# One attention, mixture and tanhshrink kernel: the weight decode in two streams, finished tokens kept in DRAM, sums kept in PSUM, later tokens prepared in small steps

## The chip, the cores and the metric

The kernel runs on one core of one Trainium2 chip. The metric is the device time of one execution in microseconds; the kernel before takes 1109.34 us (median of three timed runs, 1107.19 to 1110.84). Engines are named as in the profile: PE (matrix multiply), DVE (vector), ACT (activation), POOL (GpSimd), SP (here only the queue that issues DMAs).

## The reference, cut to what matters

Three stages follow each other. All data are float32, and the last two weight matrices arrive as float64.

```python
# 1: two attentions, 4 batches x 8 heads, 576 tokens, head size 64, 32 packed queries
p_packed = softmax_attention(p, k, v)
x = softmax_attention(q, p_packed, p_packed)      # -> x: 2304 tokens x 512
# 2: mixture of 4 experts, 512 -> 1024 -> 512
for e in range(4):
    out += prob[:, e:e+1] * (relu(x @ w1[e]) @ w2[e])
# 3: tanhshrink network, 512 -> 2048 -> 512; w_in and w_out are float64
h = out @ w_in
result = (h - tanh(h)) @ w_out
```

## The kernel before, in words

Every float32 product is made of three PE products of rounded parts: each operand is split into a high part `h` (an ACT copy that rounds to the format PE reads) and a low part `l` (the rest, a subtraction on DVE or POOL). PE then multiplies high by high, high by low and low by high into one PSUM sum. So each tile that PE is to read costs an ACT instruction and a DVE or POOL instruction first.

**The middle stage** has two passes `p` (two batches, 1152 tokens, 9 token tiles of 128 each) and eight chunks `c` of hidden columns (half an expert each). `pack_w1` (L425, token `W`) folds the packed queries into the up weights, and forms the sums of blocks (`wsum`, `wp`) that a seven-product form of the 2x2 block multiplication needs. `up_prod` (L509, token `g`) makes, for one chunk and one batch, the hidden activations in four steps with two PSUM tiles X and Z (names `hpx`, `hpz`, two banks each, pool `ps2` of two tiles). Step 0 multiplies into X, which ACT copies out, then into Z; `done` (L535) then adds the copy to Z on DVE (L536, `p<-hpz,p`), which writes the sum to SBUF, and `split_h` (L459) applies the relu: ACT writes `h0h` (L461), DVE writes `h0l` (L462). Step 1 goes on summing in X, and begins a new sum in Z (`hpz<-th`). Step 2 does two such `done`s, one of X and one of Z (`u`), step 3 the last piece of X. `down` (L567, token `d`) multiplies one token tile's activations by the down weights, 12 PE products of 512 columns (`yps`), and DVE adds the scaled result to that tile's `x2` (L586), a tile of the 20-buffer pool `u2`. An `x2` tile lives from the first chunk of its pass until the third stage has read it, so in the second pass 18 of the 20 buffers hold `x2`.

**PE's order** is written out by hand as strings of such tokens (`EVEN`, `ODD`, `TURN`, `LASTA`, `LAST`, L60 to L70) and run in that order. DVE, ACT, POOL and SP execute what the planner gave them in the order it laid down at build time, ready work first and earlier program text first among it. Each engine takes its list strictly from the front.

**The decode** (`decode`, L363) turns the float64 bit patterns of `w_in` and `w_out` into float32 pairs and stores them in DRAM (`wing`, `wout_s`) for the third stage. It is one generator; each `_` in the strings adds `STEPS` = 1.3 to a credit, and whole credits are spent on its steps; after a load step the spending stops until the next `_`. For each of 32 blocks of 128x512 words, `words` (L334) runs one ACT copy (L338), two DVE instructions (L339, L343), an ACT square in the same step (L346), two more on DVE (L348, L352) and two on POOL (L354, L355). `w_in` blocks go in pairs through block sums (L372 to L376), then all are split and stored. The work tiles come from the 5-buffer pool `k4`, which also holds the raw down weights (`wraw`, L415) and `wsum`. A group takes two blocks of `w_in` and two of `w_out` in turn, 23 steps, and there are eight groups; the strings hold 156 `_`.

**The third stage** takes three units `u` of 768 tokens. `x_quad` (L619, token `q`) transposes three `x2` tiles for each quarter of the tokens on PE (L638, `xps`), forms the block sums T1 to T4 straight from PSUM (L644) and splits (`x_split`, L610, helper L147 and L148). For unit 0 all four quarters use the one tile of pool `psw`; for units 1 and 2 the quarters are made inside the main loop. That loop has 24 steps n of one column group each: `s3` (L685, `h3ps`) makes the seven products of group n, with ACT copies (L708) and DVE adds (L712) out of two one-bank PSUM tiles; `elem` and `elem_split` do the tanhshrink and the split; `s4` (L924, `ops`) multiplies group n-2 by `w_out` into six one-bank tiles. The quarters of unit 1 stand in step 1, those of unit 2 in steps 9 and 10; three of the seven splits of a unit follow in later steps (`late_split`).

Of the kernel before, what the change touches and what calls it, by code (L numbers as in the profile page):

```python
# [26 lines left out]
STEPS = 1.3  # L27
# [39 lines left out]
    "w0 g7110 _ d710 _ q00 g7111 _ d711 _ g7112 _ q01 d712 g7113 q02 d713 q03 d714 s0 d715 s1 d716 s2 d717 s3 d718 "  # L67
# [4 lines left out]
def kernel(  # L72
# [66 lines left out]
    cst = const.tile([128, 20], F32, name="cst")  # L139
    wing = [dram.tile([128, 2, 1792], F32, name=f"wing{i}") for i in range(8)]  # L140
# [194 lines left out]
    def words(st, lf):  # L335
# [9 lines left out]
        )  # L345
        nc.scalar.activation(out=hw.bitcast(F32), in_=hw.bitcast(F32), func=ACTF.Square)  # L346
# [16 lines left out]
    def decode():  # L363
        for i in range(8):
            w = k4t([128, 2, 512], F32R, "win")
            for b in range(2):
                st = load_words(win[2 * i + b])
                yield True
                yield from words(st, f(w[:, b]))
            a11, a12, a21, a22 = (f(w[:, b, 256 * k:256 * k + 256]) for b in range(2) for k in range(2))  # L370
            s = k4t([128, 4, 256], F32R, "wins")
            nc.vector.tensor_tensor(out=f(s[:, 0]), in0=a21, in1=a22, op=ALU.add)  # L372
            nc.vector.tensor_tensor(out=f(s[:, 1]), in0=f(s[:, 0]), in1=a11, op=ALU.subtract)
            yield
            nc.vector.tensor_tensor(out=f(s[:, 2]), in0=a11, in1=a21, op=ALU.subtract)
            nc.vector.tensor_tensor(out=f(s[:, 3]), in0=a12, in1=f(s[:, 1]), op=ALU.subtract)  # L376
            hi = k4t([128, 1024], F32R, "winh")
            for h, l in ((hi[:, 0:512], w[:, 0]), (hi[:, 512:768], w[:, 1, 256:512])):
                nc.scalar.activation(out=h, in_=f(l), func=ACTF.Copy)
                nc.gpsimd.tensor_tensor(out=l, in0=f(l), in1=f(h), op=ALU.subtract)  # L380
            yield
            nc.sync.dma_start(out=wing[i][:, 0, 0:768], in_=f(hi[:, 0:768]))
            nc.sync.dma_start(out=wing[i][:, 1, 0:512], in_=f(w[:, 0]))
            nc.sync.dma_start(out=wing[i][:, 1, 512:768], in_=f(w[:, 1, 256:512]))
            yield
            hi = k4t([128, 4, 256], F32R, "winh")
            nc.scalar.activation(out=hi, in_=f(s), func=ACTF.Copy)
            for k in (slice(0, 2), slice(2, 4)):
                nc.gpsimd.tensor_tensor(out=s[:, k], in0=f(s[:, k]), in1=f(hi[:, k]), op=ALU.subtract)
            yield  # L390
            for k, t in enumerate((hi, s)):
                nc.sync.dma_start(
                    out=wing[i][:, k, 768:1792], in_=f(t).rearrange("p a b -> p (a b)")
                )
            yield
            for b in range(2):
                st = load_words(wout[2 * i + b])
                yield True
                o = k4t([128, 2, 512], F32R, "fo")
                lf = f(o[:, 1])  # L400
                yield from words(st, lf)
                nc.scalar.activation(out=o[:, 0], in_=lf, func=ACTF.Copy)
                nc.gpsimd.tensor_tensor(out=o[:, 1], in0=lf, in1=f(o[:, 0]), op=ALU.subtract)
                yield
                nc.sync.dma_start(out=wout_s[2 * i + b], in_=f(o))


    w2h, w2l, wph, wpl, raw = {}, {}, {}, {}, {}

# [209 lines left out]
    def x_quad(u, q):  # L619
# [4 lines left out]
        def raw():  # L624
            if u == 0:
                return k4t([128, 2, HT], F32, "xr")
# [412 lines left out]
```

## Time and profile before

| | |
|---|---|
| timed runs, median | 1109.34 us |
| profiled execution, whole | 1105.16 us |
| its span, first to last instruction | 1103.3 us |
| PE busy | 1069.0 us, 97% |
| DVE busy | 877.4 us, 80% |
| ACT busy | 638.3 us, 58% |
| POOL busy | 250.9 us, 23% |
| mean granted clock of PE | 0.995 |

The profile is of one execution. Busy is the time in which an engine had an instruction under way; a wait names the instruction whose end released the waiting one; the granted clock is a share of full speed (1.0 is 2.4 GHz, 0.5 is 1.2 GHz). The ends of PE's products are modelled, so PE may be busy and yet not at its peak. An attention stage fills the first 90 us, the middle stage runs to about 690, the third stage to the end.

### The profile page before, as it was taken

The numbers are of one execution on the slowest core, as the hardware profiler recorded it, in microseconds if no ns is written. First come the engines' busy times: TensorE is split into PE (matmuls) and PEld (weight loads), VectorE is DVE, ScalarE is ACT, GpSimd is POOL, SyncE is SP. The second block draws the span as 40 slices with busy tenths as digits, with TensorE's granted clock in tenths as the row PEclk, the third lists the DMA queues.
The fourth block names the chain that finished last, engine by engine and source line by source line (L and its number), as shares of the span: only waits on it lengthen the run. The fifth ranks groups of instructions, "written<-read, shape, count | busy, mean of one in ns | idle before, by whom it ended". The sixth has DMA issues, their size and how long they took to land.

```text
span 1103.3 us, 16383 instructions
## 1 busy us (share of the span) xinstructions
PE 1069.0 (97%) x6356; PEld 904.5 (82%) x6356; DVE 877.4 (80%) x1327; ACT 638.3 (58%) x1001; POOL 250.9 (23%) x185
## 2 busy tenths in 40 slices
PE   8899999999999999989999998999999899999998
PEld 6777888888778888778887787888999789889886
DVE  4677898888897857888978776799887968778885
ACT  3456454455554455455555443577777757777675
POOL 0102153553544224445445430000000000000000
PEclk9999999999999999999999999999999899999999
DMA  9624224342444222434352413254555435565532
GB/s 343 211 65 158 94 86 151 128 171 93 166 131 168 77 77 78 163 113 143 138 178 90 147 41 134 76 190 173 205 196 200 171 130 205 191 215 187 199 124 96
DMA packets 42317, 162.84 MB, mean 148 GB/s; under 512 B 4736, under 2 KB 5760, under 8 KB 39168
## 3 DMA queue, kind: packets, MB, share of 16 engines
q1 hardware_dynamic: 42240, 161.80, 41.8%
q8 instruction: 50, 0.82, 0.3%
q14 instruction: 27, 0.22, 0.1%
HBM read 133.99 MB, written 27.79 MB: 147 GB/s over the span
## 4 chain that ended last, share of the span: by engine, by line
PE 39%; DVE 6%; ACT 2%; issue 1%; POOL 1%; DMA 1%; DVEq 0%; ACTq 0%; POOLq 0%
PE ops L937 16%; PE h3ps L699 15%; PE yps L575 5%; PE hpx L525 1%; PE hpz L525 1%; DVE xr L644 1%; DVE xl L148 1%; DVE gl L920 0%; PE xps L638 0%; DVE h1l L462 0%; DVE f L348 0%; DMA f<-in_win_dram 0%; DVE x L586 0%; DVE h L898 0%; DMA wout<-fo 0%
## 5 line engine op out<-in xcount | busy, mean ns | idle before, releaser
L937 PE MATMUL ops<-wo,gh 128*128 128x512 f32 x576 | 179.7, 393 | 1.6 <-DVE xr L644 1.5
L423 POOL TENSOR_TENSOR w2l<-wraw,w2h 128x512 fp32r<-128x512 f32 x64 | 94.3, 1494 | 210.5 <-ACT w2h L421 189.5
L937 PEld LDWEIGHTS ops<-wo,gh 128*128 128x128 f32 x576 | 107.2, 189 | 20.9 <-issue 2.3
L575 PE MATMUL yps<-w2h,h0h 128*128 128x512 f32 x288 | 118.1, 410 | 4.4 <-DVE x L586 3.0
L586 DVE SCALAR_TENSOR_TENSOR x<-yps,pn,x 128x512 f32<-128x512 f32 x126 | 93.7, 743 | 30.7 <-PE yps L575 30.3
L937 PE MATMUL ops<-wo,gl 128*128 128x512 f32 x288 | 114.0, 396 | 0.9 <-DVE gl L920 0.9
L575 PE MATMUL yps<-w2h,h0l 128*128 128x512 f32 x288 | 113.6, 395 | 0.0
L575 PE MATMUL yps<-w2l,h0h 128*128 128x512 f32 x288 | 113.3, 393 | 0.0
L575 PE MATMUL yps<-w2h,h1l 128*128 128x512 f32 x288 | 112.5, 391 | 0.6 <-DVE h1l L462 0.6
L575 PE MATMUL yps<-w2h,h1h 128*128 128x512 f32 x288 | 112.9, 392 | 0.0
L575 PE MATMUL yps<-w2l,h1h 128*128 128x512 f32 x288 | 112.2, 390 | 0.0
L699 PE MATMUL h3ps<-xh,wg 128*128 128x384 f32 x384 | 106.5, 337 | 0.6 <-DVE h L712 0.6
L525 PE MATMUL hpx<-th,wp 128*128 128x288 f32 x336 | 81.5, 298 | 4.3 <-DVE p L536 3.6
L575 PEld LDWEIGHTS yps<-w2h,h0h 128*128 128x128 f32 x288 | 54.3, 188 | 37.1 <-issue 21.0
L894 DVE TENSOR_TENSOR t<-h,t 128x768 f32<-128x768 f32 (+1 forms) x50 | 46.2, 924 | 37.9 <-ACT t L892 37.8
L699 PEld LDWEIGHTS h3ps<-xh,wg 128*128 128x128 f32 x384 | 70.3, 188 | 3.1 <-DVE h L712 0.9
L699 PE MATMUL h3ps<-xbh,wg 128*128 128x384 f32 x224 | 64.7, 346 | 5.0 <-DVE h L712 3.8
L889 ACT ACTIVATE z<-h 128x768 f32<-128x768 f32 (+1 forms) x50 | 40.8, 816 | 47.8 <-DVE h L712 47.7
L525 PEld LDWEIGHTS hpx<-th,wp 128*128 128x128 f32 x336 | 58.6, 188 | 9.8 <-DVE p L536 5.2
L575 PEld LDWEIGHTS yps<-w2h,h1l 128*128 128x128 f32 x288 | 54.1, 188 | 13.0 <-DVE h1l L462 1.1
L937 PEld LDWEIGHTS ops<-wo,gl 128*128 128x128 f32 x288 | 54.1, 188 | 12.9 <-DVE gl L920 1.3
L699 PE MATMUL h3ps<-xl,wg 128*128 128x384 f32 x192 | 64.5, 336 | 0.0
(177 smaller groups left out, 2642.0 us busy)
## 6 DMA issues: line engine op xcount, KB each, us to landing
wg<-wing SPq DMA_DIRECT2D x24, 1792.0 KB, 7.2
wraw<-in_w_dram SPq DMA_DIRECT2D x64, 512.0 KB, 4.5
wo<-wout SPq DMA_DIRECT2D x48, 512.0 KB, 5.1
f<-in_win_dram SPq DMA_DIRECT2D x16, 512.0 KB, 4.7
f<-in_wout_dram SPq DMA_DIRECT2D x16, 512.0 KB, 5.0
wout<-fo SPq DMA_DIRECT2D x16, 512.0 KB, 2.9
kt<-in_kT_dram SPq DMA_DIRECT2D x16, 288.0 KB, 5.6
qt<-in_qT_dram SPq DMA_DIRECT2D x16, 288.0 KB, 6.8
```

The source lines that it names most:

```text
L148: (eng or nc.vector).tensor_tensor(out=lo, in0=src, in1=f(hi), op=ALU.subtract)
L423: nc.gpsimd.tensor_tensor(out=l[:, k], in0=r[:, k], in1=f(h[:, k]), op=ALU.subtract)
L525: nc.tensor.matmul(out=ps[:, ff, 0:HB], lhsT=W[a][:, slot, c0], rhs=x[b], start=(start and k == 0), stop=(stop and k == 2), skip_group_che ...
L575: nc.tensor.matmul(out=ps, lhsT=a[:, ff, o:o + 128], rhs=w[c, fp][:, ff], start=(k == 0), stop=(k == 11),)
L586: last[0] = nc.vector.scalar_tensor_tensor(out=x2[tt], in0=ps, scalar=pn[:, tt, e:e + 1], in1=x2[tt], op0=ALU.mult, op1=ALU.add,).ins
L644: nc.vector.tensor_tensor(out=out[:, k], in0=src if a is None else a[:, k], in1=src if b is None else b[:, k], op=ALU.subtract,)
L699: nc.tensor.matmul(out=ps, lhsT=wg[n][:, a, slot, 128 * kk:128 * kk + 128], rhs=x[c][b][kk] if isinstance(x[c][b], list) else x[c][b][:, k ...
L889: nc.scalar.activation(out=zk, in_=hk, func=ACTF.Square)
L894: nc.vector.tensor_tensor(out=tk, in0=hk, in1=tk, op=ALU.subtract)
L937: nc.tensor.matmul(out=ps, lhsT=a, rhs=wo[n][ff][:, w], start=(i == 0 and ff == 0 and k == 0), stop=(i == NG - 1 and ff == 1 and k == 2), ...
```

## The change

Five edits go together.

1. **Decode.** The generator becomes two. Each handles every second block: first the 16 `w_out` blocks, then the 8 groups of `w_in`, 7 steps a block and 20 steps a group, 272 steps in all. Each credit goes to the other stream than the last. `words` yields once more, ahead of the ACT square. Outputs come from `u2`; only the loaded words stay in `k4`. Stores are made piece by piece (`store_split`), in two DMAs each. `STEPS` is 1.9, and a load no longer ends the spending.
2. **Finished tokens.** In the last chunk of pass 0, `down` stores each finished `x2` tile to DRAM (`xs`) and gives its buffer back; `reload` (token `l`) fetches tiles 0 to 5 at the head of `LAST`, and 6 to 8 after `d714`.
3. **Sums in PSUM.** `done` writes its sum over the PSUM tile it came from, and the relu and the split read it there; only the first `done` of step 2 still writes to SBUF, as X goes on summing.
4. **Unit 0.** The fourth quarter's transposes use a `ps2` tile, and the first group's Z uses the `psw` tile. T1 and T2 are now split with the second and third quarter, T4 and T3 with the fourth.
5. **Units 1 and 2.** A quarter is now two `x_raw` calls, each with three transposes and one ACT copy into SBUF; the sums and splits (`x_prep`) are made from there, mostly in place, in five parts over steps 3 to 7 and 11 to 15, each behind the last DVE add of the step before. Step 10 orders its `s4` parts anew.

```diff
-STEPS = 1.3
+STEPS = 1.9
+PREP = (0, 3, 11)
...
-    "w0 g7110 _ d710 _ q00 g7111 _ d711 _ g7112 _ q01 d712 g7113 q02 d713 q03 d714 s0 d715 s1 d716 s2 d717 s3 d718 "
+    "w0 l06 g7110 _ d710 _ q0 g7111 _ d711 _ g7112 _ q1 d712 g7113 q2 d713 q3 d714 l69 s0 d715 s1 d716 s2 d717 s3 d718 "
...
+    xs = [dram.tile([128, 512], F32, name=f"xs{t}") for t in range(TP)]
...
         )
+        yield
         nc.scalar.activation(out=hw.bitcast(F32), in_=hw.bitcast(F32), func=ACTF.Square)
...
+    def store_split(dst, c, t):
+        n = t.shape[-1]
+        hi = u2t([128, n], F32R, "fh")
+        nc.scalar.activation(out=hi, in_=f(t), func=ACTF.Copy)
+        yield
+        nc.gpsimd.tensor_tensor(out=t, in0=f(t), in1=f(hi), op=ALU.subtract)
+        yield
+        nc.sync.dma_start(out=dst[:, 0, c:c + n], in_=f(hi))
+        nc.sync.dma_start(out=dst[:, 1, c:c + n], in_=f(t))
+    def decode_out(blocks):
+        for i in blocks:
+            st = load_words(wout[i])
+            yield
+            t = u2t([128, 512], F32R, "fo")
+            yield from words(st, f(t))
+            yield from store_split(wout_s[i], 0, t)
+    def decode_in(groups):
+        for i in groups:
+            w = []
             for b in range(2):
                 st = load_words(win[2 * i + b])
+                yield
+                w.append(u2t([128, 512], F32R, "fi"))
+                yield from words(st, f(w[b]))
+            a11, a12, a21, a22 = (f(w[b])[:, 256 * k:256 * k + 256] for b in range(2) for k in range(2))
+            sm = [u2t([128, 512], F32R, "fs") for _ in range(2)]
+            s1, s2, s3, s4 = (f(t)[:, 256 * k:256 * k + 256] for t in sm for k in range(2))
+            nc.vector.tensor_tensor(out=s1, in0=a21, in1=a22, op=ALU.add)
+            nc.vector.tensor_tensor(out=s2, in0=s1, in1=a11, op=ALU.subtract)
             yield
+            nc.vector.tensor_tensor(out=s3, in0=a11, in1=a21, op=ALU.subtract)
+            nc.vector.tensor_tensor(out=s4, in0=a12, in1=s2, op=ALU.subtract)
             yield
+            for c, t in ((0, w[0]), (512, w[1][:, 256:512]), (768, sm[0]), (1280, sm[1])):
+                yield from store_split(wing[i], c, t)
+    streams = [
+        itertools.chain(decode_out(range(k, 16, 2)), decode_in(range(k, 8, 2))) for k in range(2)
+    ]
 
...
-        def done(ps, t, fp, half):
-            nc.vector.tensor_tensor(out=t, in0=ps[:, :, 0:HB], in1=t, op=ALU.add)
-            split_h(fp, slice(t0 + half * HB, t0 + half * HB + HB), t)
+        def done(ps, t, fp, half, keep=False):
+            o = t if keep else ps[:, :, 0:HB]
+            nc.vector.tensor_tensor(out=o, in0=ps[:, :, 0:HB], in1=t, op=ALU.add)
+            split_h(fp, slice(t0 + half * HB, t0 + half * HB + HB), o)
-            done(X, p5, 1, 1)
+            done(X, p5, 1, 1, True)
...
+        if p == 0 and c == NCH - 1:
+            nc.sync.dma_start(out=xs[tt], in_=x2.pop(tt))
+
+    def reload(a, b):
+        for t in range(a, b):
+            x2[t] = u2t([128, 512], F32, "x2")
+            nc.sync.dma_start(out=x2[t], in_=xs[t])
...
+        pl, tg = (ps2, "p2") if q == 3 else (psw[0], "pw")
+        ps = pl.tile([128, 2, 512], F32, tag=tg, name="xps")
...
+    RAW = ("B12", "B22", "B11", "B21")
+    def x_raw(u, q, k):
+        c = RAW[q]
+        kh, th = int(c[1]) - 1, int(c[2]) - 1
+        if k == 0:
+            if q < 3:
+                xr[c] = late["raw"].tile([128, 2, HT], F32, tag="xr", name="xr")
+            else:
+                xr[c] = [u2t([128, HT], F32, "xr") for _ in range(2)]
+        ps = late["ops"].tile([128, 512], F32, tag="ops", name="xps")[:, 0:HT]
+        for i in range(3):
+            c0 = 128 * (2 * kh + k)
+            nc.tensor.transpose(
+                ps[:, 128 * i:128 * i + 128], x2[6 * u + 3 * th + i][:, c0:c0 + 128], ident
+            )
+        with tc.high_priority(offset=PRIO):
+            nc.scalar.activation(out=xr[c][k] if q == 3 else xr[c][:, k], in_=ps, func=ACTF.Copy)
+    def x_prep(u, k):
+        if k == 0:
             x_tiles(u)
+            x_split(u, "B11")
+            xr["T1"] = xr["B11"]
+            x_minus("T1", "B12", "B11")
+        elif k == 1:
             x_split(u, "T1")
+            x_split(u, "B22")
+        elif k == 2:
+            xr["T2"], xr["T3"] = xr["T1"], xr["B12"]
+            x_minus("T2", "B22", "T1")
+            x_minus("T3", "B22", "B12")
+            x_split(u, "T2")
+        elif k == 3:
+            x_split(u, "B21")
+            xr["T4"] = xr["B22"]
+            x_minus("T4", "B21", "T2")
+        else:
+            x_split(u, "T4")
+            x_split(u, "T3")
...
-                xz[n] = [ps2.tile([128, 2, 512], F32, tag="p2", name="h3ps")[:, 0, 0:HT] for _ in range(2)]
+                xz[n] = [
+                    pl.tile([128, 2, 512], F32, tag=tg, name="h3ps")[:, 0, 0:HT]
+                    for pl, tg in ((ps2, "p2"), (psw[0], "pw"))
+                ]
...
             while credit[0] >= 1:
                 credit[0] -= 1
-                if next(bg, None):
-                    break
+                next(streams[0], None)
+                streams.reverse()
...
-                order[k].append(("q", 1, k))
+                order[k] += [("r", 1, k, 0), ("r", 1, k, 1)]
         if n == NG + 1:
-            order[2].append(("q", 2, 0))
-            order[3].append(("q", 2, 1))
+            order[2] += [("r", 2, 0, 0), ("r", 2, 0, 1)]
+            order[3] += [("r", 2, 1, 0), ("r", 2, 1, 1)]
         if n == NG + 2:
             order = [
-                [("s", n, 0), ("q", 2, 2)], [("s", n, 1), ("q", 2, 3)],
-                [("s", n, 2), ("o", m, range(0, 4), 0)], [("s", n, 3), ("o", m, range(4, 6), 0), ("o", m, range(6), 1)],
+                [("s", n, 0), ("r", 2, 2, 0), ("r", 2, 2, 1)],
+                [("s", n, 1), ("r", 2, 3, 0), ("r", 2, 3, 1), ("o", m, range(0, 4), 0)],
+                [("s", n, 2), ("o", m, range(4, 6), 0), ("o", m, range(0, 2), 1)], [("s", n, 3), ("o", m, range(2, 6), 1)],
             ]
+        for u in (1, 2):
+            if 0 <= n - PREP[u] < 5:
+                with tc.issue_after(summed[n - 1]):
+                    x_prep(u, n - PREP[u])
```

## Rows read from the trace of the kernel before

**Rows 1.** Windows, by stage: window; us; busy (instructions) of PE, PEld, DVE, ACT, POOL; clock; DMA.

```profile
90.00:640.00 550.00, 536.81 (x3230) 441.92 (x3231) 456.17 (x684) 281.84 (x448) 235.95 (x167) 1.00 0.37 128
...
680.00:700.00 20.00, 16.80 (x80) 14.19 (x79) 15.38 (x22) 8.92 (x15) 0.00 (x0) 0.91 0.25 93
700.00:750.00 50.00, 47.76 (x248) 42.24 (x247) 44.16 (x75) 37.53 (x67) 0.00 (x0) 1.00 0.47 174
...
845.00:880.00 35.00, 30.01 (x143) 26.37 (x142) 30.45 (x48) 28.04 (x45) 0.00 (x0) 0.90 0.55 193
880.00:1090.00 210.00, 210.00 (x1044) 188.56 (x1043) 167.86 (x226) 152.56 (x218) 0.00 (x0) 1.00 0.48 172
```

**Rows 2.** Waits of PE, whole span: who waited for whom: us in total, times, longest.

```profile
PE hpz L525 <- DVE p L536: 5.2, 7, 1.3
...
PE hpx L525 <- DVE p L536: 3.6, 3, 1.9
PE xps L638 <- DVE xl L148: 3.2, 1, 3.2
PE yps L575 <- DVE x L586: 3.0, 4, 1.0
```

**Rows 3.** Windows around one of three spells of low clock.

```profile
860.00:864.40 4.40, 4.22 (x17) 4.12 (x18) 4.40 (x8) 4.40 (x8) 0.00 (x0) 0.61 0.12 45
```

**Rows 4.** Timeline, ACT, one copy of 384 columns out of PSUM.

```profile
715.52 0.49 ACT L653 ACTIVATE xr<-xps 128x384 f32<-128x384 f32 x1 [0.51 <-issue]
```

**Rows 5.** Groups by line, DVE, form by form: line, instruction, count | busy us, mean ns | idle.

```profile
L462 DVE SCALAR_TENSOR_TENSOR h0l<-u,h0h 128x576 fp32r<-128x576 f32 x28 | 30.9, 1104 | 0.2
...
L462 DVE SCALAR_TENSOR_TENSOR h0l<-p,h0h 128x576 fp32r<-128x576 f32 x28 | 25.9, 926 | 10.0 <-ACT h0h L461 9.9
...
L462 DVE SCALAR_TENSOR_TENSOR h1l<-hpx,h1h 128x576 fp32r<-128x576 f32 x28 | 21.0, 751 | 5.3 <-ACT h1h L461 5.1
...
L148 DVE TENSOR_TENSOR xl<-xr,xh 128x768 fp32r<-128x768 f32 x6 | 5.6, 952 | 0.4 <-ACT xh L147 0.4
```

**Rows 6.** DMA issues: tiles, queue, count, KB each, median us from issue to landing.

```profile
wg<-wing SPq DMA_DIRECT2D x24, 1792.0 KB, 7.2
...
out_dram<-po SPq DMA_DIRECT2D x18, 256.0 KB, 2.1
```

**Rows 7.** Timeline, the issue of one DMA on SP's queue.

```profile
562.71 0.33 SPq L415 DMA_DIRECT2D wraw<-in_w_dram  x1
```

**Rows 8.** Line L462: count: shortest/median/longest ns, first and last start, shapes.

```profile
L462 DVE SCALAR_TENSOR_TENSOR h0l<-p,h0h x28: 745/758/1856, 93.7 to 670.8; 128x576 fp32r<-128x576 f32 x28
```

**Rows 9.** Timeline, DVE, 288 to 297 us: start, length, instruction, [idle before <-releaser].

```profile
288.39 0.43 DVE L339 TENSOR_SCALAR f<-f 128x512 uint32<-128x512 uint32 x1 [2.57 <-ACT fo L338]
...
291.86 0.75 DVE L536 TENSOR_TENSOR p<-hpz,p 128x576 f32<-128x576 f32 x1
...
294.68 1.85 DVE L462 SCALAR_TENSOR_TENSOR h0l<-p,h0h 128x576 fp32r<-128x576 f32 x1
```

**Rows 10.** Timeline, POOL, 293 to 296 us.

```profile
294.55 1.37 POOL L355 TENSOR_TENSOR fo<-fo,f 128x512 f32<-128x512 f32 x1
```

**Rows 11.** Timeline, PE, 287 to 293 us.

```profile
287.60 0.30 PE L525 MATMUL hpz<-a2h,wp 128*128 128x288 f32 x1
...
292.66 0.40 PE L525 MATMUL hpz<-th,wp 128*128 128x288 f32 x1 [0.62 <-DVE p L536]
```

**Rows 12.** Timeline, 654 to 656 us.

```profile
654.32 0.76 DVE L462 SCALAR_TENSOR_TENSOR h0l<-p,h0h 128x576 fp32r<-128x576 f32 x1 [0.75 <-ACT h0h L461]
...
655.96 0.29 PE L525 MATMUL hpz<-th,wp 128*128 128x288 f32 x1
```

**Rows 13.** Waits of ACT, whole span.

```profile
ACT f L346 <- DVE f L343: 30.6, 25, 2.8
...
ACT fo L338 <- DMA f<-in_wout_dram: 21.4, 7, 5.0
...
ACT win L338 <- DMA f<-in_win_dram: 15.0, 9, 3.6
```

More of the change, by code (lines that the diff above doesn't have):

```diff
@@ L1 @@
+import itertools
 from contextlib import ExitStack
@@ L381, in decode @@
-            yield
[L382 to L405, printed above, removed]
+                yield
@@ L608, in x_tiles, with pieces, x_minus, x_quad @@
                 xc[u][names[3 * k + i]] = [x[:, i] for x in hl]
+    def pieces(*xs):
+        if any(isinstance(x, list) for x in xs):
+            return [[x[k] if isinstance(x, list) else x[:, k] for x in xs] for k in range(2)]
+        return [xs]
     def x_split(u, c):
-        src = xr[c]
         if c not in xc[u]:
             xc[u][c] = [[u2t([128, HT], F32R, f"t4{s}") for _ in range(2)] for s in "hl"]
-            for k in range(2):
-                split(xc[u][c][0][k], xc[u][c][1][k], src[:, k])
-        else:
-            split(*xc[u][c], src)
-    def x_quad(u, q):
+        for h, l, r in pieces(*xc[u][c], xr[c]):
+            split(h, l, r)
+    def x_minus(out, a, b):
+        for o, x, y in pieces(xr[out], xr[a], xr[b]):
+            nc.vector.tensor_tensor(out=o, in0=x, in1=y, op=ALU.subtract)
+    def x_quad(q):
         c = ("B12", "B11", "B22", "B21")[q]
         kh, th = int(c[1]) - 1, int(c[2]) - 1
-        def raw():
-            if u == 0:
-                return k4t([128, 2, HT], F32, "xr")
-            return late["raw"].tile([128, 2, HT], F32, tag="xr", name="xr")
-        if u == 0:
-            ps = psw[0].tile([128, 2, 512], F32, tag="pw", name="xps")
-            dst, parts = [ps[:, k] for k in range(2)], [(slice(None), ps[:, :, 0:HT])]
-        else:
-            dst = [late["ops"].tile([128, 512], F32, tag="ops", name="xps") for _ in range(2)]
-            parts = [(k, dst[k][:, 0:HT]) for k in range(2)]
+        pl, tg = (ps2, "p2") if q == 3 else (psw[0], "pw")
+        ps = pl.tile([128, 2, 512], F32, tag=tg, name="xps")
         for k in range(2):
@@ L711, in add @@
             with tc.high_priority(offset=PRIO):
-                nc.vector.tensor_tensor(out=t, in0=ps, in1=t, op=ALU.add)
+                summed[n] = nc.vector.tensor_tensor(out=t, in0=ps, in1=t, op=ALU.add).ins
         if step == 0:
@@ L731, in s3 @@
             keep(c21, X)
-    bg = decode()
     def norm_probs():
@@ L796 @@
         "w": load_g,
+        "l": reload,
         "_": background,
@@ L855 @@
             run(TURN)
-    for _ in bg:
-        pass
+    for st in streams:
+        for _ in st:
+            pass
     pm.close()
@@ L947, in s4 @@
                 nc.sync.dma_start(out=out[r0:r0 + 128, :], in_=o)
-    late_split = {}
-    for u in (1, 2):
-        for k, t in enumerate(("T2", "T4", "T3")):
-            late_split[NG * (u - 1) + 3 + k] = ((u, t),)
     load_g(1)
```

73 lines of the change are left out of this document (24 added, 49 removed).

## The prediction

> **What bounds the kernel now.** I read the windows by stage first, then PE's waits, then the timelines behind the longest ones. In steady stretches PE is never idle: from 880 to 1090 us it is busy for all 210 us [rows 1]. The change takes no product from PE and adds none, so all that it can give is PE's idle time and PE's slow time, and these stand in four places [rows 1]: 13.2 us of the 550 us of the middle stage (550 less 536.81), 3.2 of the 20 us around 690, 2.2 of the 50 us from 700, and 5.0 of the 35 us from 845. PE's waits name DVE nearly every time [rows 2]: in the middle stage `p<-hpx` and `p<-hpz` (L536, 3.6 and 5.2 us) and `x` (L586, 3.0), around 690 the split of a quarter that frees the `psw` tile (3.2, once). After the stalls around 690 and 850 to 870 the granted clock falls: over 4.4 us it is 0.61 [rows 3], so 4.4 x 0.39 = 1.7 us of work are lost in each of three spells (the windows around 690 and 850 show the same, with 0.91 of 20 us and 0.90 of 35 us [rows 1]: 1.8 and 3.5 us). Altogether 23.6 us of idling and 5.1 us of slow clock can be won.
>
> All sums below are against the profiled execution, 1105.2 us. The median of the timed runs is 1109.3, 4.2 us above it, and I add 4.2 at the end.
>
> **The late units' tokens, and unit 0.** Units 1 and 2 lose their sums out of PSUM and gain ACT copies: 8 a unit at 0.49 us [rows 4] against two now, so 6 x 0.49 = 2.9 us of ACT more a unit, spread over a step or two in which ACT is at 73% (152.56 of 210 [rows 1]): hidden. The block sums and splits now come over five steps. They are 4 subtractions and 7 splits, 11 DVE instructions of 768 columns at 0.95 us [rows 5], 10.5 us a unit; three of the splits stood in later steps before, so about 7.6 us leave the crowded stretch. A step has 42 + 36 = 78 products, and 1044 products in 210 us [rows 1] make it 15.7 us; DVE is at 80% there, 12.6 us, so there is room for 3.1, and the fullest part (two sums, one split) takes 2.9. That is nearly full, and an add (L712) may come late behind a sum; the two PSUM tiles give it only the products in between as cover. I cost this 1.0 us for both units, with 0 and 5 as bounds. In exchange I let 0.5 of the 2.2 us after 700 stand, and 0.6 of the 5.0 us after 845 with no slow spell left: gains of 1.7 and of 4.4 + 3.4 = 7.8 us. In unit 0 the fourth quarter no longer waits for the third's splits, since it has a tile of its own in `ps2`; next late is its own split, which s3's first Z needs, so I leave 0.5 of the 3.2: 2.7 + 1.7 of clock = 4.4 us. Sum of this part: 1.7 + 7.8 + 4.4 - 1.0 = 12.9 us.
>
> **Tokens by way of DRAM.** 9 stores and 9 loads of 256 KB. A DMA of that size lands in 2.1 us [rows 6]. The stores hold a buffer that nobody needs at once. The loads at the head of `LAST` have about 20 us if the buffers come free when the decode ends, which by the count of steps (272 steps / 1.9 = 143 of the 156 `_` marks) is before `LASTA`. Cost 0; without that cover, see the third rival. With the finer stores of the decode (12 DMAs a group where there were 7, 40 more in all) SP issues 58 more at 0.33 us [rows 7], 19 us of a queue that mostly waits for buffers: 0.
>
> **Sums in PSUM: what it frees.** The split of a sum in SBUF took 1104 (`u`) and 926 ns (`p`), that of `hpx` in PSUM 751 ns [rows 5]. So 28 x 0.35 + 28 x 0.175 = 14.8 us leave DVE in the middle stage, where it is busy for 456 of 550 us [rows 1]. The excess stands in a few long ones, up to 1856 ns at a median of 758 [rows 8], and the one at 294.68 lay across a POOL instruction of the decode [rows 9, 10]. The Trainium skill's page "SBUF — State Buffer", section "SBUF: two separate sides", gives the rule: a VectorE instruction with two SBUF inputs and a GpSimd one that reads SBUF exclude each other for their whole length. The rows agree, and by it none of the 56 would be held any more. A second rule speaks against the edit: "VectorE: DVE Perf Modes", section "The TRN2 errata", has a VectorE instruction start 62 cycles later from PSUM than from SBUF (120 against 58), an estimate of 56 x 0.065 = 3.6 us more of DVE by that page's figures; the median of 758 ns from SBUF beside a mean of 751 from PSUM shows no such thing here.
>
> **Sums in PSUM: what it holds.** Now Z can't be written again when the add ends, but only when relu and split have read it. That is a longer wait of PE's step 1, and everything behind it in PE's fixed order waits too. In the worst pair Z's last product of step 0 ends at 287.90 and step 1's first starts at 292.66 [rows 11]; the add ran at 291.86, the split ended at 296.53 [rows 9]: 3.87 us too late. In a clean pair the split ends at 655.08 and Z is wanted at 655.96 [rows 12]: 0.88 to spare. Read so for all 28 pairs (splits from 93.7 to 670.8 us [rows 8]), 20 are late, by 31 us together; 5 of these go when the split takes 0.75 us. So the upper bound of this edit is 26 us of PE, if DVE and ACT keep their present lateness; the lower is 0, since in clean pairs add, relu and split fit.
>
> **Decode in two streams: what it does to that lateness.** The worst pair is late because DVE stood for 2.57 us on ACT's first decode copy, which itself waited for a load [rows 9]. Such waits at the head of ACT's queue are 21.4 and 15.0 us, and the square that waits for DVE's L343 in the same step another 30.6 us [rows 13]. Behind them wait the copies of X and Z, the relu and the copies of `wsum`, so DVE's work comes in late heaps. The new `yield` takes the square out of that step, and between two steps of one stream now always lies one of the other, where 1.3 credits often ran two in a row. A load still has about one mark until its use (2 / 1.9), as before, so those 36 us shrink but don't vanish. DVE's share of decode work per mark stays (0.85 us), as the count of marks needed does (184 / 1.3 = 142 before, 143 after).
>
> I take a third of the 26 us: 9 us of Z waits in place of 5.2 (clean pairs, of which there are eight of 28, are nearest to what an unblocked ACT gives), and 2.5 of the other 8.0 us of idling in this stage left, since a PE that waits for Z gives DVE time to catch up. 13.2 becomes 11.5: a gain of 1.7, between -26 and +13.
>
> **Sum.** 12.9 + 1.7 = 14.6; 1105.2 - 14.6 = 1090.6, and 1094.8 against the median: 1095.
>
> **The rivals.**
> - *The held Z decides* (slower side). The lateness stays; step 1 waits 26 us more. For it: 20 late pairs, and DVE at 83%. Against: each wait of PE also lets DVE catch up, and 14.8 us leave DVE. 1105.2 - 12.9 + 26 = 1118, or 1122 with the 4.2. It decides from 12.9 / 28 = 0.46 us more of waiting a pair on. Chance 0.16.
> - *The two streams clear the stage.* ACT's 67 us of decode waits mostly go, Z is free in time, 3 of the 13.2 us are left: 1105.2 - 12.9 - 10.2 = 1082, or 1086. For it: the clean pairs, all where the decode rests. Against: loads still have one mark. Chance 0.20.
> - *The reload comes late.* If SP issues the loads behind the first `wg` load, their 1.5 MB at that load's rate (1792 KB in 7.2 us [rows 6]) are 6.2 us, and unit 0's transposes wait that long with a slow spell behind: 7.9 us; 1098.5, or 1103. Against: SP issues what is ready, and `wg` must wait for its buffer. Chance 0.08.
> - *The sums only move the stalls.* DVE, filled to 15.5 of 15.7 us, is late with the adds in ten steps, and half of the 9.5 us of the late units comes back: 1095.4, or 1100. For it: PE's present stalls there are just such adds. Chance 0.12.
>
> The first forecast has 0.44, with a range of its own of 1088 to 1104. From the same cases: this kernel's runs can tell no change within 0.3%, 1106 to 1112.7. The held Z ends above that with 0.12 and within it with 0.04; the rest puts 0.05 within it and 0.01 above. So faster 0.78, same 0.09, slower 0.13. The range of 1083 to 1113 leaves out the far part of the second rival and that of the first.
>
> **What would show it.** In the changed kernel's profile: no wait of `xps` at the end of the middle stage and no clock below 1.0 there; PE busy for nearly all of the stretch in which unit 2's quarters are made; `h0l` splits all at about 750 ns; `hpz<-th` waiting for the split (L462's successor) rather than the add, about 9 us in all; ACT's waits for the square gone. It is wrong if those Z waits exceed 20 us, if transposes wait for DMA, or if adds of the third stage stall PE in steps 3 to 7 or 11 to 15.

## The result, and the profile after

The changed kernel takes 1121.63 us (median; 1119.81 to 1123.39), the kernel before beside it 1108.26 (1106.68 to 1110.84): ratio 1.0118, 95% interval 1.0091 to 1.0145. It is slower by 13 us, where 1095 was forecast and the range ended at 1113. The profiled execution took 1121.19 us, its span is 1119.4.

The windows by stage, in the columns of [rows 1]:

```profile
90.00:640.00 550.00, 522.05 (x3093) 428.83 (x3092) 418.18 (x659) 268.75 (x435) 212.15 (x157) 0.98 0.36 125
680.00:700.00 20.00, 20.00 (x111) 17.43 (x110) 10.54 (x15) 5.41 (x9) 0.00 (x0) 1.00 0.25 93
700.00:750.00 50.00, 49.22 (x270) 44.08 (x269) 36.87 (x61) 33.07 (x62) 0.00 (x0) 1.00 0.43 159
845.00:880.00 35.00, 32.86 (x174) 29.55 (x173) 26.11 (x36) 27.56 (x45) 0.00 (x0) 1.00 0.61 220
880.00:1090.00 210.00, 208.11 (x1040) 187.00 (x1039) 176.50 (x239) 157.27 (x230) 0.00 (x0) 1.00 0.50 179
```

The middle stage got worse twice over: PE idles for 28.0 us of the 550 instead of 13.2, and the clock is 0.98 where it was 1.00. The reader should not compare the other windows row by row, since the kernel after reaches each point some 20 us later. For that I set the same product of both traces side by side (the n-th `yps`, the first `h3ps` of a step) and took the difference of their times after the span's start (a pair is the X and Z of one chunk and one batch):

```
point                          after - before, us
first pair of X and Z                  +1.4
11th pair of 28, its step 1           +18.1
15th pair, the first of pass 1        +24.6
28th pair, the last before unit 0     +27.2
third stage, step 0                   +22.2
third stage, step 3                   +20.2
third stage, step 10                  +20.0
third stage, step 11                  +15.8
end                                   +15.9
```

So the change did two things. It lost 25.8 us from the first pair to the last (27.2 - 1.4), 23.2 of them in pass 0, and it won 11.4 us behind that: 5.0 around unit 0, 2.2 up to step 10, 4.2 where unit 2's tokens are made.

PE's waits, whole span (against [rows 2]; columns as there):

```profile
PE hpz L527 <- DVE h0l L464: 22.2, 17, 2.8
PE hpx L527 <- ACT p L534: 3.5, 2, 2.3
PE h3ps L740 <- ACT h L749: 2.5, 2, 2.0
PE qtp L321 <- DVE wp L440: 2.3, 1, 2.3
PE ops L978 <- ACT xr L687: 1.9, 1, 1.9
```

The waits of `xps` and of `hpz` for the add are gone, and one wait has taken their place: Z for the split that reads it, 22.2 us in 17 times. The windows over the low-clock spells of the middle stage (columns of [rows 3]) show the rest:

```profile
159.50:162.90 3.40, 3.40 (x12) 2.92 (x12) 2.53 (x3) 2.03 (x3) 2.02 (x2) 0.51 0.05 18
224.40:231.20 6.80, 5.61 (x16) 4.74 (x17) 3.02 (x6) 1.70 (x3) 3.99 (x4) 0.50 0.01 2
354.10:357.50 3.40, 3.40 (x9) 2.64 (x9) 0.00 (x0) 1.00 (x2) 2.36 (x2) 0.50 0.02 7
388.20:391.60 3.40, 3.40 (x10) 2.62 (x9) 1.74 (x5) 0.49 (x1) 0.00 (x0) 0.51 0.30 118
582.80:586.20 3.40, 3.40 (x9) 2.64 (x8) 2.20 (x1) 2.58 (x5) 3.40 (x3) 0.50 0.60 230
```

For 20.4 us PE ran at half clock (1.2 GHz), which costs 10.2 us; before, this stage had no such spell. Four of them follow a wait of 2.1 to 2.4 us by 0.3 to 1.3 us: of Z behind the products of 156.6, 350.4 and 579.0, of the transposes behind that of 384.7. The double one follows a wait of `hpx` of 2.32 us (up to 222.27) and begins within a wait of Z of 2.25 us (up to 225.59). Not every such wait has a spell behind it: the two longest of Z, 2.58 us at 308 and 2.79 us at 479, have none. So 14.8 us more of idling (28.0 - 13.2) and 10.2 us of clock make 25.0 of the 25.8 us that the table shows.

How Z comes to wait is seen in one pair. Timeline of PE, then of ACT (the copy of X that the add needs, and the Relu), then of DVE, from Z's last product of step 0 to its first of step 1:

```profile
304.32 0.30 PE L527 MATMUL hpz<-a2h,wp 128*128 128x288 f32 x1
...
307.89 0.29 PE L527 MATMUL hpx<-th,wp 128*128 128x288 f32 x1
310.76 0.40 PE L527 MATMUL hpz<-th,wp 128*128 128x288 f32 x1 [2.58 <-DVE h0l L464]
```

```profile
304.69 0.63 ACT L534 ACTIVATE p<-hpx 128x576 f32<-128x576 f32 x1
...
309.27 0.65 ACT L463 ACTIVATE h0h<-hpz 128x576 fp32r<-128x576 f32 x1 [1.46 <-DVE hpz L539]
```

```profile
304.60 1.39 DVE L352 SCALAR_TENSOR_TENSOR f<-f 128x512 f32<-128x512 f32 x1
305.90 2.33 DVE L456 TENSOR_TENSOR wp<-wsum,wp 128x1024 fp32r<-128x1024 f32 x1
308.15 0.42 DVE L356 TENSOR_SCALAR f<-f 128x512 uint32<-128x512 uint32 x1
308.48 0.75 DVE L539 TENSOR_TENSOR hpz<-hpz,p 128x576 f32<-128x576 f32 x1
309.15 0.73 DVE L589 SCALAR_TENSOR_TENSOR x<-yps,pn,x 128x512 f32<-128x512 f32 x1
309.95 0.76 DVE L464 SCALAR_TENSOR_TENSOR h0l<-hpz,h0h 128x576 fp32r<-128x576 f32 x1
```

Z is complete at 304.6, and the copy of X at 305.3. DVE is not idle, and it does not wait for a load: it works its list. A step of the decode, the subtraction of the next unit's weights (L456) and another decode step stand ahead of the add, which so begins 3.9 us after Z is complete and 3.2 us after the copy; in the kernel before, Z was free when the add ended, and now the Relu and the split come on top of it. From these rows, an estimate: an add at 305.3 with Relu and split right behind it (0.75, 0.65 and 0.76 us) would let Z go at 307.5, ahead of the 308.2 at which PE wants it.

Two terms of the forecast can be read from the groups. The splits of sums (count: shortest/median/longest ns, first to last start), against [rows 8]:

```profile
L464 DVE SCALAR_TENSOR_TENSOR h0l<-hpz,h0h x56: 740/756/759, 95.1 to 708.0; 128x576 fp32r<-128x576 f32 x56
```

None is held any more, where the longest had been 1856. The rule of the Trainium skill that the prediction drew on ("SBUF — State Buffer", section "SBUF: two separate sides") agrees with that. And ACT's waits at the head of its list, against [rows 13]:

```profile
ACT f L350 <- DVE f L346: 14.3, 13, 3.8
...
ACT fi L341 <- DMA f<-in_win_dram: 13.1, 5, 4.2
ACT fo L341 <- DMA f<-in_wout_dram: 9.1, 6, 5.5
```

67 us have become 36.5. The two streams did shrink what the prediction had named as the source of the lateness, and yet Z waited. Nor was ACT free for it: the Relu's waits for DVE's sums grew from 60.9 us (with 2.0 for `u`) to 104.9. Before, then after:

```profile
ACT h1h L461 <- DVE p L536: 43.5, 21, 3.7
ACT h0h L461 <- DVE p L536: 15.4, 14, 2.4
```

```profile
ACT h1h L463 <- DVE p L539: 77.4, 23, 5.6
ACT h0h L463 <- DVE hpz L539: 27.5, 22, 3.4
```

### The profile page after: what moved, and what is told of

The parts are those of the page before. It is cut to its first block, busy times and chain, and to the rows that moved or that the text cites. A ratio compares the mean times of both kernels' runs of the same rounds, so it can differ in the third digit from the quotient of the medians.

```text
span 1119.4 us, 16558 instructions
## 1 busy us (share of the span) xinstructions
PE 1074.3 (96%) x6356; PEld 909.0 (81%) x6356; DVE 855.5 (76%) x1317; ACT 641.3 (57%) x1017; POOL 239.1 (21%) x185
## 4 chain that ended last, share of the span: by engine, by line
PE 69%; DVE 12%; ACT 7%; DMA 6%; issue 3%; POOL 1%; SPq 1%; DVEq 0%; ACTq 0%; POOLq 0%
PE yps L578 22%; PE ops L978 16%; PE h3ps L740 15%; PE hpx L527 4%; PE hpz L527 4%; DMA f<-in_wout_dram 3%; PE hps L479 2%; PE wps L432 2%; DVE x L589 1%; DMA f<-in_win_dram 1%; DVE f L352 1%; DVE h0l L464 1%; PE qsc L279 1%; PE pv L257 1%; DVE hpz L539 1%
## 5 line engine op out<-in xcount | busy, mean ns | idle before, releaser
L425 POOL TENSOR_TENSOR w2l<-wraw,w2h 128x512 fp32r<-128x512 f32 x64 | 85.1, 1351 | 270.1 <-ACT w2h L423 245.2
L578 PEld LDWEIGHTS yps<-w2h,h0l 128*128 128x128 f32 x288 | 55.2, 192 | 12.5
L578 PEld LDWEIGHTS yps<-w2h,h1h 128*128 128x128 f32 x288 | 55.3, 192 | 12.1
L578 PEld LDWEIGHTS yps<-w2l,h1h 128*128 128x128 f32 x288 | 55.0, 191 | 12.3
```

The source lines that it names most:

```text
L425: nc.gpsimd.tensor_tensor(out=l[:, k], in0=r[:, k], in1=f(h[:, k]), op=ALU.subtract)
L578: nc.tensor.matmul(out=ps, lhsT=a[:, ff, o:o + 128], rhs=w[c, fp][:, ff], start=(k == 0), stop=(k == 11),)
```

## The experiments

All ratios are to the kernel before, run beside each kernel. Times of different groups of runs may differ by 1 or 2 us for that alone: the kernel before had medians of 1106.66 to 1108.84. A trace is of one execution; where that one lies far from the median, it is said.

**Taking the sums out of PSUM again.** The first two kernels differ from the changed one in one word or two:

```diff
-            done(Z, t, 0, 0)
+            done(Z, t, 0, 0, True)      # e1, e3: sum of step 0 to SBUF
...
-            done(Z, u, 0, 1)
+            done(Z, u, 0, 1, True)      # e1 only: sum of u to SBUF too
```

> The changed kernel with all sums written to SBUF again, as before the change; everything else as changed. Theory 'held Z' (PE's step 1 waits until relu and split have read the sum in Z: 22.2 us of waits in the changed kernel, and five spells of low clock in the middle stage, some 10 us): the waits fall back to about 5 us and the spells go, 1121.6 - 17 - 10 = about 1095 us (1090 to 1100). Rival 'decode' (the two streams, or the DRAM round of the tokens, make DVE and ACT late): the time stays above 1112.

> The changed kernel with the one sum in SBUF whose Z tile is wanted again at once (the first done, of step 0); the sum of step 2 (u) stays in PSUM, where nothing wants the tile for some 8 us. Held Z: as the kernel with all sums in SBUF or up to 5 us less, 1089 to 1097 us, since 28 splits stay free of POOL. Decode rival: above 1112.

e1 took 1104.62 us, ratio 0.9966 [0.9943, 0.9990]; e3 1101.85, 0.9955 [0.9929, 0.9981]. Both lie above the range that was expected (the paragraph on e6 and e1 takes up what is left) and far below the rival's 1112. So the held Z of step 0 costs 19.8 us (e3; 18.0 by the ratios), more than the whole loss. It is the held tile and not another order of DVE's work: from the first pair to the last, DVE runs the same 716 instructions in both traces, in the same order but for three swaps of neighbours. u's sum in PSUM costs nothing; e3 is 2.8 us faster than e1 in the median, but 1.2 by the ratios, whose intervals overlap. In e3 the Z waits for h0l are gone (PE's waits):

```profile
PE hpx L527 <- ACT p L534: 3.9, 2, 2.6
...
PE hpz L527 <- DVE p L539: 3.0, 3, 1.5
```

**The same edit in the kernel before (e2).** `done` as in the changed kernel, nothing else.

```diff
-            nc.vector.tensor_tensor(out=t, in0=ps[:, :, 0:HB], in1=t, op=ALU.add)
+            o = t if keep else ps[:, :, 0:HB]
+            nc.vector.tensor_tensor(out=o, in0=ps[:, :, 0:HB], in1=t, op=ALU.add)
...
-            done(X, p5, 1, 1)
+            done(X, p5, 1, 1, True)
```

> The kernel before with one edit alone: sums kept in PSUM. Held Z: hpz waits for the split by 20 to 30 us and the clock falls in the middle stage, 1108.3 + 26 to 36 = 1134 to 1144 us. Decode rival: within 4 us of the kernel before, 1104 to 1112.

1114.69 us, 1.0088 [1.0059, 1.0117], with PE's longest wait

```profile
PE hpz L525 <- DVE h0l L462: 21.7, 14, 3.4
```

The edit hurts in the old kernel too, so the new decode is no condition for it, but by some 8 us in the median, far less than was expected. The trace, with almost the same 22 us of waits, is of the slowest execution (1121.30 us, mean granted clock 0.988); the other four took 1114.16 to 1118.02 us at 0.992 to 0.995.

**Writing Z later (e4).** Z's new product of step 1 goes to the head of step 2, so that Z may be held longer:

```diff
         elif step == 1:
...
-            mul(Z, 3, cmb(0), True, False)
-            prod[bi].append(kept(Z, "p5"))
         elif step == 2:
-            X, Z, u, p5 = prod[bi]
+            X, Z, u = prod[bi]
+            mul(Z, 3, cmb(0), True, False)
+            p5 = kept(Z, "p5")
```

> The changed kernel with all its sums in PSUM, but the product that begins anew in Z moved from step 1 to the head of step 2 in PE's order, one down product (2.75 us) later. Held Z: most of the 22 us goes, though PE may now wait for ACT's copy of that product (the copy p), up to 0.4 us a pair: 1090 to 1103 us. Decode rival: above 1112.

1109.01 us, 1.0020 [1.0006, 1.0033]. 12.6 us come back, less than was expected, since a new wait appears: Z's second product of the step may be added only when ACT has copied the first, just made:

```profile
PE hpz L527 <- ACT p L534: 11.6, 9, 3.1
```

**The tokens' edits alone (e6).** Edits 4 and 5 in the kernel before; sums in SBUF, one decode stream, nothing by way of DRAM.

```diff
+PREP = (0, 3, 11)
...
-    "w0 g7110 _ d710 _ q00 g7111 _ d711 _ g7112 _ q01 d712 g7113 q02 d713 q03 d714 s0 ..."
+    "w0 g7110 _ d710 _ q0 g7111 _ d711 _ g7112 _ q1 d712 g7113 q2 d713 q3 d714 s0 ..."
...                                # x_quad, x_raw, x_prep, s3 as in the change
```

> The kernel before with the edits of the tokens alone (unit 0's fourth quarter in its own tile; units 1 and 2 copied raw and summed in place over later steps); decode, sums and resident tokens as before. In the changed kernel these edits gain 10 us (25.8 us behind before unit 0, 15.8 behind after unit 2). If they stand alone: 1106.7 - 10 = 1097 us (1094 to 1099), so that decode and DRAM edits together cost some 7 us. Rival (they need the freed buffers, or the decode edits are neutral): 1103 to 1107.

1096.73 us, 0.9910 [0.9887, 0.9932]: 10 us faster. The differences to the kernel before, taken as in the table above, are +1.1 at the first pair, +3.9 at the last, -1.1, -3.1, -3.3 and -7.9 at steps 0, 3, 10 and 11, -7.8 at the end: gains of 5.0, 2.2 and 4.6 in the three places, next to the 5.0, 2.2 and 4.2 of the whole change. Two of the windows of [rows 1] in this kernel:

```profile
680.00:700.00 20.00, 19.82 (x108) 17.25 (x107) 17.62 (x24) 9.55 (x16) 0.00 (x0) 1.00 0.26 93
...
845.00:880.00 35.00, 32.84 (x164) 28.97 (x163) 26.12 (x34) 30.77 (x49) 0.00 (x0) 0.95 0.54 188
```

**The same with u's sum in PSUM (e8).**

```diff
-            done(Z, u, 0, 1, True)
+            done(Z, u, 0, 1)
```

> The kernel before with the edits of the tokens, and with the one sum in PSUM whose tile nobody wants soon (u, step 2). Between the all-SBUF and this form of the changed kernel lay 2.8 us: 2 to 3 us below the kernel with the tokens' edits alone, 1093 to 1096. Rival (the 28 splits off POOL's way change nothing that PE waits for): the same within 1 us.

1093.34 us, 0.9869 [0.9842, 0.9896]. Against e6 this gains 3.4 us, and the four runs of each lie apart (1090.72 to 1094.36, 1096.00 to 1099.17): this is what u's sum in PSUM is worth where nobody waits for the tile. The 28 splits of it take 749 ns in the mean, where e6 has 1104; that the gain comes from this alone was not tried.

**The DRAM round alone (e12).** Edit 2 in the kernel before.

```diff
+        if p == 0 and c == NCH - 1:
+            nc.sync.dma_start(out=xs[tt], in_=x2.pop(tt))
...                                # reload, l06 and l69 as in the change
```

> The kernel before with one edit alone: pass 0's finished tokens stored to DRAM and fetched again at the head and in the middle of LAST. If DRAM costs nothing, 1105 to 1109 us, and the 7.9 us between the tokens' edits alone (1096.7) and the changed kernel with its sums in SBUF (1104.6) belong to the two streams. Rival (SP held up by the stores, or a late fetch): 1111 or more.

1107.03 us, 0.9990 [0.9970, 1.0010]: it costs nothing that the runs can tell.

**What the two streams cost, and a longer lead.** The decode and the DRAM round are all that separates e1 from e6, and e1 is 7.9 us slower (5.4 in the traces). The differences to the kernel before, in us, show where:

```
point                                e1      e6
15th pair, the first of pass 1    +10.6    +1.6
28th pair                          +4.6    +3.9
third stage, step 0                -0.5    -1.1
third stage, step 10               -2.6    -3.3
third stage, step 11               -2.7    -7.9
end                                -2.4    -7.8
```

So the two streams lose 9 us in pass 0 and win nearly all of it back by step 10. What stays stands where unit 2's tokens are made: e1 lacks e6's gain there. PE waits for the raw copies, which it does not in e6, and two half-clock spells of 3.4 us stand there (at 855.3 and 869.0) instead of one:

```profile
PE ops L978 <- ACT xr L687: 3.3, 1, 3.3
```

e3 and e5 lack most of this gain too, while the changed kernel has it; what decides it was not tried. It hides a part of the held Z's price: e3 is 23.4 us ahead of the changed kernel at step 10, and 19.2 at the end. In pass 0 of e1's trace ACT stands on a load for its longest time, and the next unit's weights wait behind it:

```profile
206.46 0.39 ACT L449 ACTIVATE wp<-wps 128x256 fp32r<-128x256 f32 x1 [0.76 <-DVE wp L448]
213.31 0.66 ACT L341 ACTIVATE fo<-f 128x512 f32<-128x512 uint32 x1 [6.46 <-DMA f<-in_wout_dram]
213.87 1.04 ACT L455 ACTIVATE wp<-wsum 128x1024 fp32r<-128x1024 f32 x1
```

So I gave each load two more steps of its stream until its use, with the first sum in SBUF (e5) and with all sums in PSUM (e7):

```diff
-STEPS = 1.9
+STEPS = 2.35
...
             st = load_words(wout[i])      # and in decode_in
             yield
+            yield
+            yield
```

> The changed kernel with its first sum in SBUF, and with each decode load given two more steps until its first use (336 steps in all, STEPS 2.35, so that the decode ends at the same mark). Theory 'late loads' (pass 0 is 9 us slower than in the kernel before since ACT's list stands at the head for two loads at once): pass 0's stalls go, 1101.9 - 6 to 9 = 1093 to 1096 us. Rival (the rhythm of the two streams itself, both in step, fills DVE's list at one time): 1100 to 1105, or slower since a stream now often takes two steps at one mark.

> The changed kernel, all its sums in PSUM, with the same lead for the decode loads (STEPS 2.35). If the price of the held Z is the lateness that late loads make: 1121.6 falls to 1108 or less. Rival (the price is DVE's own queue behind each W, with loads in time or not): 1115 or more.

e5 took 1093.22 us, 0.9875 [0.9852, 0.9897]; e7 1125.20, 1.0164 [1.0143, 1.0184]. The lead gains 8.6 us where Z is free (e3 to e5), and nothing where it is held (1121.6 to 1125.2), so that with the lead the held Z costs 32.0 us: more time for the loads does not take its price away. Why the lead gains is not settled. ACT's waits for loads are 24.4 us in e5 and 24.0 in e3, no shorter; its waits for POOL's decode steps fell from 24.7 to 17.1 and DVE's for the first copy of a block from 7.9 to 3.1.

**The decode's share of DVE.** In the changed kernel (e10) and in e3 (e11) the four decode instructions of a block on DVE are left out; the square and POOL's two steps then read what ACT wrote, so that in the decode ACT no longer waits for DVE. In short:

```diff
-        nc.vector.tensor_scalar(out=lw, in0=hw, scalar1=3, ...)
-        nc.vector.scalar_tensor_tensor(out=lw, in0=hw, ...)
...
-        nc.vector.scalar_tensor_tensor(out=lw..., scalar=MIN_HI_SQ, ...)
-        nc.vector.tensor_scalar(out=hw, in0=lw, ...)
```

> The changed kernel, all its sums in PSUM, with DVE's four instructions on each decode block left out (so the weights of the third stage are not the reference's). DVE loses 3.0 us a block, 96 us in all. If the price of the held Z is made by the decode's share of DVE's queue: its Z waits fall from 22 to below 6 us, and it stands within 5 us of the same kernel with the first sum in SBUF. Rival (made by the sums of each W and by the order of DVE's list alone): still over 10 us apart.

> The same with the first sum in SBUF: DVE's four decode instructions left out. The partner of the kernel above; 1085 to 1095 us, since most of the middle stage's 14 us of idle time goes with DVE's queue. The difference of the two is the price of the held Z without the decode on DVE.

e10 took 1104.65 us, 0.9968 [0.9941, 0.9995]; e11 1087.97, 0.9796 [0.9767, 0.9825]. They are 17 and 14 us faster without that work, and still 16.7 us apart, with DVE's 588 instructions from the first pair to the last in the same order in both. DVE was busy for 355 of the 550 us (65%) in e10, and yet:

```profile
90.00:640.00 550.00, 529.95 (x3189) 436.97 (x3190) 354.62 (x552) 277.34 (x453) 223.71 (x168) 1.00 0.38 131
...
PE hpz L515 <- DVE h0l L452: 19.9, 14, 2.5
```

The decode's share of DVE is not the price either.

**What stands ahead in the lists.** This leaves the order, and the rest of DVE's work. The subtraction L456 and ACT's copy before it (L455), which finish the next unit's weights, are needed only a unit later, but for the first unit of each pass, which takes its weights in its own step 1. e13 moves these two behind the add and split of step 0, in the changed kernel; e14 and e15 do the same in e5 and e8, where Z is not held.

```diff
-        nc.scalar.activation(out=h[:, 3:7], in_=s, func=ACTF.Copy)
-        nc.vector.tensor_tensor(out=l[:, 3:7], in0=s, in1=f(h[:, 3:7]), op=ALU.subtract)
+        rest_w.append((h, l, s))      # both are issued by finish_w
...
             done(Z, t, 0, 0)
+            finish_w()                # behind last[0] and last[1]
```

> The changed kernel with one thing moved: of each unit's next weights, the copy of the four sums to the high half (ScalarE) and the subtraction for the low half (VectorE, 128x1024) are put behind the add and the split of step 0, instead of ahead of them. All sums stay in PSUM. Theory (the held Z pays for what stands ahead of its add in the two lists): the waits of hpz for h0l fall from 22.2 us in 17 to under 8, the half-clock spells of the middle stage from five to two at most, and the time to 1100 to 1108 us. Rival (the chain add, Relu, split with its hand-overs is too long by itself): hpz waits 15 us or more and the time stays at 1115 or above. Second rival (the weights' product is the next to be late): hpz waits fall, a wait of hpx or hpz for wp of 5 us or more takes their place, and the time is 1112 to 1122.

> The version with the longer lead of the loads and the sum of step 0 in SBUF (1093.2 us), with the same move of the next weights' last two steps behind the split. Here Z is let go after the add alone, and PE's waits for hpz were 1 us in all. Theory: the move is worth something only where Z is held, so this one gains 0 to 3 us, 1090 to 1094. Rival (the move clears the two lists for everything else as well): 1088 or less.

> The kernel before with the tokens' edits and the sum of u in PSUM (1093.3 us), one stream of decode, with the same move. Theory: within 3 us of 1093.3, as nothing waited there for a held Z of step 0. Rival (the move clears the lists for everything else): 1089 or less; and if its copy and subtraction, put later, delay the next unit's products, over 1097.

e13 took 1112.65 us, 1.0049 [1.0030, 1.0068]; e14 1099.81, 0.9928 [0.9901, 0.9954]; e15 1100.28, 0.9946 [0.9930, 0.9962]. PE's waits in e13:

```profile
PE hpz L538 <- DVE h0l L475: 9.6, 10, 1.9
PE hpx L538 <- ACT p L545: 3.3, 2, 2.2
...
PE hpx L538 <- DVE wp L467: 2.0, 2, 1.1
...
PE hpx L538 <- ACT wp L466: 1.4, 1, 1.4
```

The Z waits fall from 22.2 to 9.6 us; new waits for `wp` take 3.4 us. The time falls by 9.0 us (7.6 by the ratios), less than the theory had asked for. The trace is of the fastest of ten executions (1107.00 us, mean granted clock 0.992), and has one spell of 6.8 us left of the five in the middle stage. The other nine took 1110.53 to 1114.01 us at 0.986 to 0.991, and the changed kernel runs at 0.984 to 0.989: in most executions the move took idling away and little of what the clock costs.

The move also has a price of its own: where Z is free it costs 6.6 (e5 to e14) and 6.9 us (e8 to e15; 5.9 and 8.5 by the ratios). Part of it is the first unit of each pass, whose weights now come late. In e14 both waits for L471 stand there, the second with a half-clock spell behind it (425.3 to 428.7):

```profile
PE hpx L542 <- DVE wp L471: 3.4, 2, 2.3
```

```profile
97.28 0.53 PE L542 MATMUL hpx<-th,wp 128*128 128x288 f32 x2 [1.08 <-DVE wp L471]
424.73 0.54 PE L542 MATMUL hpx<-th,wp 128*128 128x288 f32 x2 [2.31 <-DVE wp L471]
```

So the place of two instructions in two lists makes some 9 of the 17 to 20 us that the held Z costs (16.7 by e10 and e11, 19.8 by e3); about 15.8 if the move's own price (6.6 to 6.9) is added. That the two add up is an assumption, and the lead, which gained 8.6 us without the held Z and nothing with it, shows that such sums need not hold. What makes e13's last 9.6 us of waits was not taken apart, nor ACT's copy moved without DVE's subtraction.

**The best version, once more (e9).** e5's longest wait of PE is the one of `ops` for the raw copies of unit 2, which stands in e1 and e3 too, at 3.3 us (PE's waits, then ACT's timeline):

```profile
PE ops L982 <- ACT xr L691: 3.8, 1, 3.8
```

```profile
856.74 0.84 ACT L959 ACTIVATE gh<-h 128x768 fp32r<-128x768 f32 x1 [2.37 <-DVE h L943]
857.49 0.83 ACT L934 ACTIVATE z<-h 128x768 f32<-128x768 f32 x1
858.23 0.83 ACT L937 ACTIVATE t<-h 128x768 f32<-128x768 f32 x1
858.96 0.85 ACT L691 ACTIVATE xr<-xps 128x384 f32<-128x384 f32 x2
```

e9 gives half of the outputs of units 0 and 1 a buffer of their own, in case those buffers held the copies up:

```diff
-                o = u2t([128, 512], F32, "po")
+                if u < 2 and t % 2 == 0:
+                    o = late["po"].tile([128, 512], F32, tag="po", name="po")
+                else:
+                    o = u2t([128, 512], F32, "po")
```

> The kernel with the lead for the decode loads and the first sum in SBUF (1093.2 us), in which PE still waits 3.8 us for the copies of unit 2's last raw quarter and 2.0 us for an s3 copy, with a spell of low clock behind. Half of the finished output tiles of units 0 and 1 get a buffer of their own instead of one of u2. Theory 'short of buffers' (the copies run 8.3 us after their transposes since they wait for a free u2 buffer): the 3.8 us and the spell (1.7) go, 1088 to 1090 us. Rival (they stand behind other work in ACT's list, whatever is free): 1092 to 1094.

1092.46 us, 0.9837 [0.9819, 0.9855], and the wait is still 3.8 us: it is not these buffers. The copies stand in ACT's list behind three instructions of 0.83 us, of which the first waited 2.37 us for DVE. e5, e8 and e9 are the best versions that leave nothing out, within 1 us of each other, and 14 to 18 us faster than the kernel before by their ratios.

## Why the prediction was wrong

- **The step that failed** is "I take a third of the 26 us: 9 us of Z waits in place of 5.2". The bound it was taken from was nearly right: 20 late pairs and 26 us were counted from the trace of before, and 17 waits of 22.2 us came. The third was argued from eight clean pairs as "nearest to what an unblocked ACT gives". ACT's decode waits did shrink (67 us became 36.5), and it did not matter: its Relu then stood longer behind DVE's sums. e3 shows that the held Z cost 19.8 us; e7 and e10 show that neither less lateness of the loads nor less decode on DVE takes that price away, and by e13 the place of two instructions in the lists makes some 9 us of it. What makes the rest is open, and why the eight pairs were clean was not tried.
- **A term was missing.** The Z waits were priced as idling alone. With four of them, and one of the transposes, came 3.4 to 6.8 us at half clock: 10.2 us more. The prediction had priced such spells where they stood in the trace of before, and not where its own new waits would make them.
- The middle stage was to gain 1.7 us and lost 25.8. The rest of it: hpx and the transposes idled for 5.8 us (3.5 and 2.3), where 2.5 was said for all other idling. By its own sign (wrong if the Z waits exceed 20 us) the prediction failed at 22.2.
- **Two streams**: counted as a help. By e1 against e6 they lose 9 us in pass 0 and win nearly all of it back by step 10, with the DRAM round in them, which costs nothing by itself (e12): no help, and not the loss. ACT's waits for the square were to go, and 14.3 of 30.6 us stayed.
- **The splits**: about 750 ns was forecast, 756 is the median. That u's sum gains 3.4 us (e8) and step 0's loses 17 to 20 (32 with the lead) separates the two halves of that edit: the gain and the cost of sums in PSUM were both real, and could have been had apart.
- **Unit 0**: 4.4 forecast, 5.0 measured, 5.0 in e6. **The first steps**: 1.7 and 2.2. **Unit 2's tokens**: 7.8 and 4.2; of 5.0 us of idling, 0.6 was to stay, and 3.9 did, in two waits for ACT (2.0 of `h3ps`, 1.9 of `ops` for the raw copies): cover was counted for DVE's adds and not for ACT's new copies. **The sums in ten steps**, priced at 1.0: no such loss is seen, the differences at steps 3 and 10 are 0.2 us apart.
- **The DRAM round**: 0 forecast, 0 measured; its loads took 7.4 us from issue to landing and PE waited for none. The third rival is out.
- **The rival "the held Z decides"** had the right end: 1122 forecast, 1121.63 measured, but not by its own sum. It had 26 us more of Z waits and no clock; it was 17.0 more of Z waits (22.2 less 5.2), 10.2 of clock, and 11.4 instead of 12.9 from the tokens. That the two sums meet is luck. At a chance of 0.16 it was held too low: of its two arguments against, that 14.8 us leave DVE came true and did not help.

## What to carry to other kernels

Price a tile that is held for one more reader by what stands ahead of that reader in its engine's fixed list: count it pair by pair from the trace, and do not take a discount because an engine will be less busy or less blocked; here neither took the price away, and moving two instructions took about half of it. Where a trace shows half-clock spells behind waits of TensorE, price such spells for the new waits of an edit too. An edit of one form in several places (here three sums) may pay in one and cost in another; ask of each which buffer it holds and who wants it next. Before a difference of two kernels is put down to one stage, follow it through the same points to the end: here 9 us lost in one pass came back in the next, and the rest stood in another stage.

## What the hardware showed that I had not expected

- Half-clock spells came in lengths of 3.4 or 6.8 us, behind waits of 2.1 to 2.4 us in an otherwise busy stretch, while waits of 2.58 and 2.79 us in the same trace had none. The double one came with two waits close together, 2.32 us up to 222.27 and 2.25 us up to 225.59, and began at 224.4, within the second.
- Waits alone do not fix the clock: e10's trace has 19.9 us of Z waits in 14 (longest 2.5) and one spell of 3.4 us in the middle stage, against five in the changed kernel, at a mean granted clock of 0.998; the other nine executions of e10 had 0.989 to 0.997. So one trace does not tell a kernel's clock.
- A split with one input in PSUM took 740 to 759 ns in all 56 places, and one with both inputs in SBUF up to 1856: the longest time fell, and the median (756 and 758) did not rise.
